# A planner that lets DVE's scales take turns with POOL, unit 0 ahead of unit 1 at the start, and new orders

## The chip, the cores and the metric

One core of one Trainium2 chip. The metric is the device time of one execution in microseconds. TensorE is called PE, VectorE DVE, ScalarE ACT, GpSimd POOL and SyncE SP. DVE's and POOL's elementwise work, ACT's activations, PE's matmuls and the DMA queues run side by side and wait for one another through semaphores.

## The reference, cut to what matters

Linear attention with a decay for each head (4 batches, 8 heads, 768 positions, 64 channels), then a feed-forward layer of width 2048 over the 3072 tokens of 512 channels:

```python
intra = np.einsum('bhic,bhjc->bhij', qb, kb) * Dmask[None]
intra = np.einsum('bhij,bhjd->bhid', intra, vb)
inter = np.einsum('bhid,bhde->bhie', qb * lam_pow[None], kv_state)
out[:, :, sl] = intra + inter
kv_state = lam_block * kv_state + np.einsum('bhsd,bhse->bhde', kb * rev_pow, vb)
...
h = x @ w_in                       # x: the attention's result, (3072, 512)
g = h + np.sin(alpha * h) ** 2 / (alpha + 1e-09)
return g @ w_out
```

## The kernel before, in words

The sequence is cut into blocks of 128 positions; two blocks of one batch are a unit, and there are 12. For each unit q, k and v come as float32 over SP's queue: in halves of four heads (256 KB) for units 0 and 1, whole (512 KB) for the others, into three buffers of each, so unit u's load waits until unit u-3's is used up. `uscale` (L504) turns each half into bfloat16: q and v are multiplied by powers of lambda (L523, "a scale"), k is only cast (L509). k and q are then transposed: by PE with a copy by DVE or ACT (`upiece_T`, L531) for units 0 to 3, by a DMA transpose on SP's queue (`upiece_D`, L552) from unit 4 on. `urun` (L583) issues the attention's small matmuls (L578) for units 0 to 3: S (scores of four heads, then masked by DVE into Smu, L658), Z (the new state: DVE keeps it in Zs, L669 and L671, and a cast Zu, L674, goes to PE), O (the outputs, which DVE or ACT writes to xT, L688). `upair` (L695) does all three for a whole unit from unit 4 on, the O of the unit before beside the S and Z of the next ("a paired piece").

Two units make a chunk of 512 tokens, six in all. For a chunk, an A-unit makes 128 rows of h from the first weights w1: four matmuls of 512 columns (`unit_A`, L811), or, as a half unit (`unit_A2`, L845), eight of 256 columns for 256 rows and half the tokens. Then ACT takes the sine (L821 or L855), ACT or POOL squares it (L825 and L859 on ACT, L826 and L860 on POOL), and DVE adds it to h into gT (L828 or L863). A B-unit (`unit_B`, L876) is four matmuls of gT with the second weights w2; four B-units make 128 tokens of output, which ACT copies (L890) and stores.

The weights come through POOL's queue as float32 and land as bfloat16, in pieces of a quarter: D0 to D3 for w1 (D0 is missing: its two halves, ws0 and ws256, come as float32 over SP's queue and are cast by `cast_w1_first`, W0 and W256, L424), E0 to E3 for w2. The text calls D1, D2, D3 weight pieces 1, 2, 3; E0 is the piece that the first B-units read. Each has a gate, written behind the colon in HEAD: `D3:v11` is issued once v of unit 1, half 1, has landed. Unit 2's loads wait for D3.

The program is made by a planner, `_Plan`. PE's and SP's instructions are issued in the order of the tables, except that the planner may take one of the next 40 on PE if it is ready sooner; ACT, DVE and POOL take whatever its model says is ready first, and where an operation names several engines (a scale, a square, an xT copy) the one that ends first, with a handicap for some. The durations are written beside each operation. From this the planner fixes every engine's order once; on the chip each engine runs its list in that order. Where PE would wait in the first 26 us the planner puts in spin matmuls (L950), which compute nothing that is used.

Two tables set the rest: HEAD (L437) is the start, with `lk00` the load of k of unit 0, half 0, `k00:DVE` its scale and engine, `Tk00` its transpose, `S0`, `Z0`, `O0`, `X0` the pieces of attention, `F:` the order of the free PSUM banks. ORDER (L899) is what follows: `h0.1.6` a half unit of chunk 0, half 1, rows of 6 and 7; `a0.4` an A-unit; `b0.2.0` a B-unit; `g` the next piece of attention; `s` skips a bank. Before, the loads, scales and DMA transposes of later units were called by a rule of their own (`ahead`, L980).

## Time and profile before

| | us |
|---|---|
| median of 3 runs | 216.63 |
| lowest, highest | 216.14, 216.72 |
| profiled execution | 216.58 |
| its span | 214.8 |
| busy: PE, DVE, ACT, POOL | 205.0, 136.6, 143.5, 93.9 |
| spin matmuls, part of PE's | 11.2 |
| PE idle from 25 to 60, 60 to 90, 90 to 200 | 0.98, 2.28, 0.07 |

The span is what the profiler saw of instructions. A group's row gives the line, the engine, the operation, output and inputs with their shapes and a count; behind the bar stand its busy time, the mean of one in ns, and the time that the engine was idle just before, with what ended it. The granted clock of TensorE is full throughout.

### The profile page before, as it was taken

Reading aid. Unit: us, or ns where it says so; the run is one execution under the profiler, and the core shown is the slowest. Engines: PE = TensorE matmul, PEld = TensorE weight load, DVE = VectorE, ACT = ScalarE, POOL = GpSimd, SP = SyncE. Lnnn points to the kernel's source line nnn. Section 1 sums busy time; section 2 is a strip of 40 time slices with the busy share of each in tenths; the row PEclk is TensorE's granted clock in tenths of the full one; section 3 lists DMA queues with packets and bytes.
Section 4 is the critical chain, followed back from the end, with each engine's and each line's share of the span. In section 5 each row is a group of like instructions: output and inputs, shape, how many; then the busy total and the mean of one; then the engine's idle time right before and its main releaser. Section 6 shows DMA issues by size and latency. Waiting matters only on the chain.

```text
span 214.8 us, 5435 instructions
## 1 busy us (share of the span) xinstructions
PE 205.0 (95%) x2290; PEld 114.9 (53%) x2290; DVE 136.6 (64%) x225; ACT 143.5 (67%) x264; POOL 93.9 (44%) x106
## 2 busy tenths in 40 slices
...
GB/s 108 298 309 234 206 255 258 252 265 344 297 202 289 271 179 318 178 283 218 277 251 268 99 49 101 2 42 62 0 52 49 0 0 3 0 2 49 52 146 148
DMA packets 62986, 34.45 MB, mean 160 GB/s; under 512 B 18273, under 2 KB 60017, under 8 KB 62961
## 3 DMA queue, kind: packets, MB, share of 16 engines
...
q0 software_dynamic: 3696, 3.67, 10.3%
...
## 4 chain that ended last, share of the span: by engine, by line
PE 78%; DMA 11%; POOL 3%; SPq 3%; ACT 2%; issue 1%; DVE 0%; POOLq 0%
PE bank L876 38%; PE bank L811 18%; PE bank L845 13%; PE bank L578 7%; DMA w<-in_moe_w_in_dram 5%; DMA k<-in_k_dram 3%; SPq L385 3%; DMA q<-in_q_dram 3%; POOL u L826 2%; PE bank L539 1%; POOL w L385 1%; ACT t L821 1%; POOL qkv L523 1%; ACT osb L890 0%; DVE gT L828 0%
## 5 line engine op out<-in xcount | busy, mean ns | idle before, releaser
L876 PE MATMUL bank<-w,gT 128*128 128x512 bf16 (+1 forms) x400 | 89.6, 371 | 1.0 <-ACT osb L890 0.7
L876 PEld LDWEIGHTS bank<-w,gT 128*128 128x128 bf16 x400 | 38.0, 98 | 41.6 <-ACT osb L890 1.2
L828 DVE SCALAR_TENSOR_TENSOR gT<-u,rinv,bank 128x512 bf16<-128x512 bf16 x56 | 40.7, 744 | 22.0 <-ACT u L825 13.4
L811 PE MATMUL bank<-xT,w 128*128 128x512 bf16 x224 | 53.1, 379 | 0.8 <-DVE gT L828 0.5
L821 ACT ACTIVATE t<-bank,alpha 128x512 bf16<-128x512 f32 x56 | 37.4, 685 | 12.2 <-PE bank L811 11.4
L863 DVE SCALAR_TENSOR_TENSOR gT<-u,rinv,bank 128x256 bf16<-128x256 bf16 x80 | 34.3, 475 | 12.8 <-POOL u L860 7.3
L845 PE MATMUL bank<-xT,w 128*128 128x256 bf16 x320 | 38.7, 273 | 0.2 <-DVE gT L828 0.2
L855 ACT ACTIVATE t<-bank,alpha 128x256 bf16<-128x256 f32 x80 | 32.9, 474 | 6.6 <-PE bank L845 5.0
L811 PEld LDWEIGHTS bank<-xT,w 128*128 128x128 bf16 x224 | 21.5, 98 | 25.7 <-DVE gT L828 1.0
L845 PEld LDWEIGHTS bank<-xT,w 128*128 128x128 bf16 x320 | 30.5, 98 | 8.2 <-ACT xT L788 1.5
L860 POOL TENSOR_TENSOR u<-t 128x512 bf16<-128x512 bf16 x25 | 26.0, 1056 | 17.8 <-ACT t L855 17.7
L826 POOL TENSOR_TENSOR u<-t 128x512 bf16<-128x512 bf16 x19 | 20.2, 1069 | 29.9 <-ACT t L821 19.6
L890 ACT COPY osb<-bank 128x512 f32<-128x512 f32 (+1 forms) x25 | 14.2, 568 | 21.9 <-PE bank L876 21.9
L767 DVE TENSOR_TENSOR Smu<-bank,masku 128x1024 bf16<-128x1024 f32 x16 | 18.9, 1219 | 13.6 <-PE bank L578 13.6
L825 ACT ACTIVATE u<-t 128x512 bf16<-128x512 bf16 x37 | 23.3, 630 | 1.8 <-DVE gT L828 0.6
L523 POOL TENSOR_TENSOR qkv<-v,Lv 128x512 bf16<-128x512 f32 x15 | 17.4, 1167 | 12.8 <-PE bank L578 10.9
L523 POOL TENSOR_TENSOR qkv<-q,Lq 128x512 bf16<-128x512 f32 x13 | 15.0, 1159 | 11.5 <-DMA q<-in_q_dram 11.5
L788 ACT CAST xT<-bank 128x512 bf16<-128x512 f32 x14 | 9.8, 740 | 9.5 <-PE bank L578 9.5
L950 PE MATMUL bank<-masku,ident 128*128 128x512 bf16 x33 | 11.2, 452 | 2.7 <-DVE masku L461 2.7
L658 DVE TENSOR_TENSOR Smu<-bank,masku 128x1024 bf16<-128x1024 f32 x8 | 9.7, 1223 | 3.3 <-PE bank L578 3.2
L509 ACT CAST qkv<-k 128x512 bf16<-128x512 f32 x11 | 6.8, 617 | 6.0 <-DMA k<-in_k_dram 6.0
L578 PE MATMUL bank<-qkT,Zu 64*64 64x128 bf16 x160 | 10.3, 221 | 0.3
...
## 6 DMA issues: line engine op xcount, KB each, us to landing
...
k<-in_k_dram SPq DMA_DIRECT2D x10, 512.0 KB, 6.5
q<-in_q_dram SPq DMA_DIRECT2D x10, 512.0 KB, 7.2
v<-in_v_dram SPq DMA_DIRECT2D x10, 512.0 KB, 8.0
w<-in_moe_w_out_dram POOLq DMA_DIRECT2D x4, 512.0 KB, 9.4
w<-in_moe_w_in_dram POOLq DMA_DIRECT2D x3, 512.0 KB, 11.4
...
```

Of the source, the lines that this page charges most:

```text
L523: emit = lambda e: e.tensor_tensor(dst, src, tab, ALU.mult)
L578: ins = e.matmul(to, w, x, start=(b, c) not in seen, stop=True, skip_group_check=True)
L811: ins = e.matmul(ps[hb][:, c0:c1], w1[:, kc, 128 * m:128 * (m + 1)], xT[x][:, kc, c0:c1], start=(kc == 0 and c0 == lo), stop=(kc == NKC - ...
L821: op("ACT", lambda e: e.activation(t16[ju][:, w], ps[hb][:, w], ACTF.Sin, scale=alpha[:, m:m + 1]), 0.69 * f, [bank(hb), "alpha"], [("t16" ...
L825: lambda e: (e.activation(u16[ju][:, w], t16[ju][:, w], ACTF.Square) if e is nc.scalar else e.tensor_tensor(u16[ju][:, w], t16[ju][:, w], ...
L826: e.tensor_tensor(u16[ju][:, w], t16[ju][:, w], t16[ju][:, w], ALU.mult)), 0,
L828: op("DVE", lambda e: e.scalar_tensor_tensor(out=gT[g][:, m, w], in0=u16[ju][:, w], scalar=rinv[:, m:m + 1], in1=ps[hb][:, w], op0=ALU.mul ...
L845: ins = e.matmul(ps[hb][:, 256 * i:256 * i + 256], w1[:, kc, 128 * (m + i):128 * (m + i + 1)], xT[x][:, kc, lo:lo + 256], start=(kc == 0 a ...
L855: op("ACT", lambda e, i=i: e.activation(t16[ju][:, 256 * i:256 * i + 256], ps[hb][:, 256 * i:256 * i + 256], ACTF.Sin, scale=alpha[:, m + ...
L860: e.tensor_tensor(u16[ju][:, :], t16[ju][:, :], t16[ju][:, :], ALU.mult)), 0,
L863: op("DVE", lambda e, i=i: e.scalar_tensor_tensor(out=gT[g][:, m + i, lo:lo + 256], in0=u16[ju][:, 256 * i:256 * i + 256], scalar=rinv[:, ...
L876: ins = e.matmul(ps[ob][:, w], gT[g][:, m, 128 * s4:128 * (s4 + 1)], w2[:, m, w], start=(m == 0), stop=(m == NM - 1),)
```

## The change

1. In the planner, the scales and k casts on DVE (`port = True`) may not run while POOL runs anything, nor POOL beside one of them: each starts only when the other's last has ended. This holds in the planner's model; on the chip nothing is added, only the choice of engine and the order follow from it.
2. HEAD is new: all loads of unit 0 but one come ahead of unit 1's, q first; ws0, the first half of the first weights, is loaded in the middle; the transposes of unit 1 are four single ones; both casts of the first weights go to DVE; D3 is gated by v of unit 0, D1 and D2 by ws0. The bank order is new.
3. ORDER is new. Loads (`l`), scales (`p`) and DMA transposes (`d`) of later units are tokens in it; 46 half units and 50 whole ones take the place of 40 and 56. Handicaps for ACT and DVE (`late_by`) are read from a token `G:` of HEAD. A few durations and landing times of the model are corrected.

```diff
+        ends = {"POOL": 0.0, "DVE": 0.0}
+        def free(o, e):
+            return max(clock[e], ends["DVE"] if e == "POOL" else ends["POOL"] if e == "DVE" and o.port else 0.0)
...
-                    _, e, d = min((max(r, clock[e]) + d + late, e, d) for e, d, late in o.given)
-                    c = (max(r, clock[e]), index[o], o, e, d)
+                    _, e, d = min((max(r, free(o, e)) + d + late, e, d) for e, d, late in o.given)
+                    c = (max(r, free(o, e)), index[o], o, e, d)
...
+            if e == "POOL" or e == "DVE" and o.port:
+                ends[e] = clock[e]
...
-            HEAD = """lk00 lv00 lq00 lk01 k01:POOL lv01 lq01 v01:POOL q00:POOL lk10 k00:DVE Tk00:7ACT lq10 lk11 Tq00:6DVE
+            HEAD = """lq01 lq00 lk00 lk01 k00:POOL q00:POOL lv00 Tk00:5DVE lv10 lv01 lq10 lw0 D1:w0 lk10 Tq00:6DVE
...
-                    long = {"POOL": 1.05 if u > 1 else 1.1, "DVE": 0.68}
+                    long = {"POOL": 1.04, "DVE": 0.68}
...
+                o.port = True
...
-                op((("POOL", 1.05 * f, 0.0), ("ACT", 0.6 * f, 0.2)),
+                op((("POOL", 1.05 * f, 0.0), ("ACT", 0.62 * f, late_by[0])),
...
-                while ahead and ahead[0][0] <= done:
-                    ahead.pop(0)[1]()
...
+                elif kind == "l":
+                    load_unit(next(loads), "kqv")
+                elif kind == "p":
+                    uprep(next(preps))
+                elif kind == "d":
+                    u = next(turns)
+                    upiece_D(u, "k")
+                    upiece_D(u, "q")
```

POOL at the start, from its first scale on. `q32_0` is q of unit 0, `q32_1` of unit 1; `w1` and `w2` are weight pieces; `dma_uv01` is the landing of v of unit 0, half 1, `dma_ws0` and `dma_ws256` of the two small loads of first weights. Before:

```order
L523 TENSOR_TENSOR qkv<-q32_0,Lq 128x2x4x64 [waits dma_uq00,done_ACT]
L509 CAST qkv<-k32_0 128x2x4x64 [waits dma_uk01]
L523 TENSOR_TENSOR qkv<-v32_0,Lv 128x512 [waits dma_uv01,done_ACT]
L523 TENSOR_TENSOR qkv<-q32_0,Lq 128x2x4x64 [waits dma_uq01]
L674 CAST Zu_0<-Zs 128x256 [waits done_DVE]
L385 DMA w1<-in_moe_w_in_dram 128x4x512 [waits dma_uq11]
L385 DMA w2<-in_moe_w_out_dram 128x4x512
L385 DMA w1<-in_moe_w_in_dram 128x4x512 [waits dma_uv11]
```

The changed POOL at the same place:

```order
L532 TENSOR_TENSOR qkv<-q32_0,Lq 128x2x4x64 [waits dma_uq01,done_ACT]
L532 TENSOR_TENSOR qkv<-q32_0,Lq 128x2x4x64 [waits dma_uq00]
L518 CAST qkv<-k32_0 128x2x4x64 [waits dma_uk00]
L532 TENSOR_TENSOR qkv<-v32_0,Lv 128x512 [waits dma_uv01,done_ACT]
L532 TENSOR_TENSOR qkv<-q32_1,Lq 128x2x4x64 [waits dma_uq10]
L393 DMA w1<-in_moe_w_in_dram 128x4x512
L393 DMA w1<-in_moe_w_in_dram 128x4x512 [waits dma_ws0]
L518 CAST qkv<-k32_1 128x2x4x64 [waits dma_uk10]
```

Unit 0's v and unit 1's first q now stand ahead of the first weight pieces; the piece with no wait of its own is D3, the next D1. Before, D1 came first, then E0, then D3.

PE at its first big matmuls, behind the first A-unit (a half unit) and the first output of unit 1. `xT_0` is the attention's result for chunk 0, `Smu_3` the last masked scores of unit 1, `masku,ident` a spin matmul. Before:

```order
L578 MATMUL bank<-Smu_3,qkv 64x128 [waits done_DVE]
L578 MATMUL bank<-Smu_3,qkv 64x128 x15
L578 MATMUL bank<-qkT,Zu_1 64x128 x2
L578 MATMUL bank<-qkT,Zu_1 64x128 [waits done_PE]
L578 MATMUL bank<-qkT,Zu_1 64x128
L845 MATMUL bank<-xT_0,w1 128x256 [waits done_ACT]
L845 MATMUL bank<-xT_0,w1 128x256 x7
L845 MATMUL bank<-xT_0,w1 128x256 [waits dma_w11,done_DVE]
L845 MATMUL bank<-xT_0,w1 128x256 x23
L811 MATMUL bank<-xT_0,w1 128x512 [waits done_DVE]
```

The changed PE there:

```order
L588 MATMUL bank<-Smu_3,qkv 64x128 [waits done_DVE]
L588 MATMUL bank<-Smu_3,qkv 64x128 x15
L588 MATMUL bank<-qkT,Zu_1 64x128 x2
L588 MATMUL bank<-qkT,Zu_1 64x128 [waits done_PE]
L588 MATMUL bank<-qkT,Zu_1 64x128
L962 MATMUL bank<-masku,ident 128x512 x4
L855 MATMUL bank<-xT_0,w1 128x256 [waits done_DVE,done_ACT]
L855 MATMUL bank<-xT_0,w1 128x256 x7
L821 MATMUL bank<-xT_0,w1 128x512 [waits dma_w11]
L821 MATMUL bank<-xT_0,w1 128x512 x3
```

Four spins now stand ahead of the second A-unit (a half unit), and the third, a whole one, waits for weight piece 1 (`dma_w11`); before, the third was a half unit that waits for the same piece, with no spin in between.

DVE in chunk 1's first A-units. `q32_2`, `k32_2` and `v32_2` are the third of three buffers, with unit 5 in them here; `gT_1` is chunk 1's g. Before:

```order
L863 SCALAR_TENSOR_TENSOR gT_1<-u16_1,rinv,bank 128x256
L523 TENSOR_TENSOR qkv<-q32_2,Lq 128x2x4x64 [waits dma_uq2]
L828 SCALAR_TENSOR_TENSOR gT_1<-u16_3,rinv,bank 128x512 [waits done_ACT]
L828 SCALAR_TENSOR_TENSOR gT_1<-u16_2,rinv,bank 128x512 [waits done_POOL]
L523 TENSOR_TENSOR qkv<-v32_2,Lv 128x512 [waits dma_uv2]
L828 SCALAR_TENSOR_TENSOR gT_1<-u16_0,rinv,bank 128x512 [waits done_ACT]
```

The changed DVE at the same place:

```order
L873 SCALAR_TENSOR_TENSOR gT_1<-u16_1,rinv,bank 128x256
L518 CAST qkv<-k32_2 128x2x4x64 [waits dma_uk2]
L873 SCALAR_TENSOR_TENSOR gT_1<-u16_2,rinv,bank 128x256 [waits done_POOL]
L873 SCALAR_TENSOR_TENSOR gT_1<-u16_2,rinv,bank 128x256
L873 SCALAR_TENSOR_TENSOR gT_1<-u16_3,rinv,bank 128x256 [waits done_POOL]
```

The two scales are gone from between the sums; a k cast is there instead. In the whole program DVE keeps two scales of 20, both in the start, and POOL has 46 where it had 28; ACT has 40 squares for 52.

82 lines of the change are left out of this document (41 added, 41 removed).

## The prediction

> **What bounds the kernel now.** I read the busy time by stretches first, since TensorE (PE) is busy 95% of the span and only its gaps can be won. Columns: stretch in us, its length, busy us of PE, PEld (weight loads), DVE, ACT, POOL, granted clock, DMA share, GB/s.
>
> ```profile
> 25.00:60.00 35.00, 34.02 (x420) 19.85 (x418) 27.76 (x47) 24.12 (x46) 20.71 (x22) 1.00 1.12 272
> 60.00:70.00 10.00, 8.66 (x87) 4.44 (x87) 8.49 (x15) 8.90 (x16) 7.71 (x9) 1.00 1.27 248
> ...
> 80.00:90.00 10.00, 9.06 (x216) 5.24 (x205) 6.40 (x8) 6.05 (x11) 4.62 (x5) 1.00 1.12 242
> 90.00:200.00 110.00, 109.93 (x1110) 60.91 (x1109) 69.29 (x112) 80.42 (x146) 43.02 (x46) 1.00 0.41 92
> ```
>
> From 90 to 200 PE idles 0.07 us: nothing there gets shorter without less PE work. The chain of work that ended last (start, us, what) gives that work by units:
>
> ```profile
> 90.23 0.87 PE bank L845 x8
> ...
> 92.83 0.86 PE bank L811 x4
> ```
>
> A half unit of eight matmuls lasts as long as a whole one of four, so six more of the one kind for six fewer of the other change PE's work by nothing. What can change is when useful work starts, 0.98 us of gaps from 25 to 60, 1.34 in the sixties, 0.94 in the eighties. Then I read the groups by line (the second number behind the bar is the mean in ns):
>
> ```profile
> L821 ACT ACTIVATE t<-bank,alpha 128x512 bf16<-128x512 f32 x56 | 37.4, 685 | 12.2 <-PE bank L811 11.4
> L855 ACT ACTIVATE t<-bank,alpha 128x256 bf16<-128x256 f32 x80 | 32.9, 474 | 6.6 <-PE bank L845 5.0 <-POOL qkv L523 1.3
> L860 POOL TENSOR_TENSOR u<-t 128x512 bf16<-128x512 bf16 x25 | 26.0, 1056 | 17.8 <-ACT t L855 17.7
> L523 POOL TENSOR_TENSOR qkv<-v,Lv 128x512 bf16<-128x512 f32 x15 | 17.4, 1167 | 12.8 <-PE bank L578 10.9 <-DMA v<-in_v_dram 1.9
> ```
>
> POOL's scales average 1.17 where the shortest rows have 1.04. The timeline (start, us, engine, line) shows why: scales of DVE and POOL that overlap run one behind the other.
>
> ```profile
> 53.84 1.04 POOL L523 TENSOR_TENSOR qkv<-q,Lq 128x512 bf16<-128x512 f32 x1
> 53.95 1.48 DVE L523 TENSOR_TENSOR qkv<-q,Lq 128x512 bf16<-128x512 f32 x1
> 54.84 1.49 POOL L523 TENSOR_TENSOR qkv<-v,Lv 128x512 bf16<-128x512 f32 x1
> ```
>
> DVE's scale ends at 55.43, 0.55 after POOL's first; POOL's second ends 0.90 after that. In the sixties such a pair stands in front of work that PE waits for:
>
> ```profile
> 59.17 6.22 PE L811 MATMUL bank<-xT,w 128*128 128x512 bf16 x28
> ...
> 63.98 1.20 DVE L523 TENSOR_TENSOR qkv<-v,Lv 128x512 bf16<-128x512 f32 x1
> 64.60 1.49 POOL L523 TENSOR_TENSOR qkv<-v,Lv 128x512 bf16<-128x512 f32 x1
> ...
> 65.90 1.04 PE L811 MATMUL bank<-xT,w 128*128 128x512 bf16 x4 [0.52 <-DVE gT L828]
> ...
> 67.34 0.44 PE L578 MATMUL bank<-qkv 64*64 64x64 bf16 x16 [0.40 <-DVE gT L863]
> ```
>
> **The sixties.** Between PE's first A-unit of chunk 1 and the paired piece of unit 4, I count what each order gives each engine, at these durations. Before: three half units and eight whole ones, 10.2 us of PE, against ACT 11.7, DVE 10.2 (three scales in it), POOL 9.9. Changed: six half, four whole and a B-unit, 10.3 of PE, against ACT 9.8, DVE 8.7 (no scale), POOL 11.3 (six scales, the last two needed only later). From 59.17 to 67.34 PE took 8.17 us for eight units worth 6.9; the piece then waits 0.4 and twice 0.2 more: 2.0 us lost. With ACT and DVE below PE most of this goes; for POOL, which stays above, I leave 0.5 lost: **-1.5**.
>
> **POOL's load.** 18 scales leave DVE and 12 squares leave ACT for POOL: 18 x 1.04 + 12 x 1.06, some 31 us on 93.9. In the sixteen A- and B-units from the 41st on, its count is 16.4 us against PE's 15.7, and squares stand behind pairs of scales (2.08). The trace shows no POOL that full beside a PE without gaps. Bounds: nothing (four buffers between ACT and POOL take it up; less than nothing isn't possible, since the relief is counted above) and 0.7 for the excess plus 0.8 for a square behind a pair. I take **+0.4**, near the low end, as both counts of ACT and DVE are smaller there. In the eighties PE waits mostly for ACT's copy of an output; ACT has some 10 us less to do, and I take back half of the 0.94: **-0.4**.
>
> **The head.** Useful work starts at 19.84, is continuous from 22.08, and stops twice:
>
> ```profile
> 19.84 1.04 PE L845 MATMUL bank<-xT,w 128*128 128x256 bf16 x8
> 22.08 3.73 PE L845 MATMUL bank<-xT,w 128*128 128x256 bf16 x32
> 31.38 1.04 PE L876 MATMUL bank<-w,gT 128*128 128x512 bf16 x4 [0.36 <-DVE gT L863]
> 34.69 0.61 PE L539 MATMUL bank<-ident,qkv 128*128 128x128 bf16 x8 [0.55 <-ACT qkv L509]
> ```
>
> The changed start I walk by hand. First the loads (7th and 9th in the queue of SP, then the 13th, a ws; then POOL's weight pieces, issue and us to landing; the last two are steps of the chain):
>
> ```profile
> 10.87 0.62 ACT L509 CAST qkv<-k 128x512 bf16<-128x512 f32 x1 [2.86 <-DMA k<-in_k_dram]
> 12.67 0.62 ACT L509 CAST qkv<-k 128x512 bf16<-128x512 f32 x1 [1.19 <-DMA k<-in_k_dram]
> 16.87 1.05 ACT L424 CAST w<-ws 128x1024 bf16<-128x1024 f32 x1 [0.67 <-DMA ws<-in_moe_w_in_dram]
> 13.89 0.94 POOL L385 DMA_DIRECT2D w<-in_moe_w_in_dram  x1 [2.19 <-DMA q<-in_q_dram]
> w<-in_moe_w_in_dram POOLq DMA_DIRECT2D x1, 512.0 KB, 7.9
> 15.56 11.39 DMA w<-in_moe_w_in_dram
> 26.97 6.94 DMA k<-in_k_dram
> ```
>
> A load lands every 0.9 us, a ws takes 1.5. Weight pieces land at 21.8 (13.89 + 7.9) and, the third, at 26.95: 2.55 apart. The second engine of the walk is DVE:
>
> ```profile
> L658 DVE TENSOR_TENSOR Smu<-bank,masku 128x1024 bf16<-128x1024 f32 x8 | 9.7, 1223 | 3.3 <-PE bank L578 3.2
> L688 DVE CAST xT<-bank 128x512 bf16<-128x512 f32 x4 | 2.8, 725 | 1.5 <-PE bank L578 1.5
> L509 DVE CAST qkv<-k 128x512 bf16<-128x512 f32 x3 | 1.3, 434 | 0.5 <-DMA k<-in_k_dram 0.5
> L669 DVE COPY Zs<-bank 128x256 f32<-128x256 f32 x2 | 0.9, 426 | 0.9 <-PE bank L578 0.9
> L548 ACT COPY qkT<-bank 128x512 bf16<-128x512 bf16 x1 | 0.6, 568 | 0.0
> ```
>
> In the new order the second v of unit 0 is the 7th load, 10.9; POOL ends it at 11.95 and unit 1's first q at 12.97, and only then issues weight piece 3, then piece 1. DVE: two Smu (1.22) from 10.95 to 13.4, two state copies to 14.2, the cast W0 (twice a k cast, an estimate of 0.85) to 15.05, xT to 15.8. This frees the bank for unit 1's k transposes; ACT's copy (0.57) and the score follow at 16.95, Smu_2 ends at 18.6, the scale of v at 19.3, unit 1's state at 20.3. The first A-unit uses the state's bank: **20.3**. Ahead of the second stand Smu_3 (to 21.5), W256 (22.4; its ws, the last load, should be there by 21.3 beside piece 3) and xT (23.1): **23.2**. Piece 3 is issued 0.92 earlier than the first piece was, but into the same bytes, so I leave the landings where they were: 3 near 21.8, piece 1 at 24.35, piece 2 at 26.95. The third unit waits for piece 1; the third to fifth run from 24.35 to 24.35 + 3 x 0.87 = 26.95, and the sixth needs piece 2: **27.0**. Before, five units from 19.84 and 22.08 on brought the sixth to 25.6: 1.4 late. Then something comes back: piece 3 releases unit 2's loads, at 21.8 and not at 26.97. Its k, 6.9 us later, is there at 29 and even four us later still ahead of its transposes, due some 9 us after the sixth unit; so the stops of 0.36 and 0.55 go. That leaves 0.5, and I add 0.1 for squares held up behind POOL's issues: **+0.6**.
>
> The unknown is how unit 2's loads and pieces 2 and E0 slow each other. Below: not at all, and DVE's chain 0.6 shorter, as its estimates allow: 0. Above: as the last two pieces of before, which ran beside them:
>
> ```profile
> 30.35 0.81 POOL L385 DMA_DIRECT2D w<-in_moe_w_out_dram  x1
> 34.19 0.81 POOL L385 DMA_DIRECT2D w<-in_moe_w_out_dram  x1 [1.68 <-DMA k<-in_k_dram]
> w<-in_moe_w_out_dram POOLq DMA_DIRECT2D x2, 512.0 KB, 9.1
> ```
>
> They land near 39.5 and 43.3, 3.8 apart: 1.25 more than 2.55 for each of two pieces, +2.5 on 0.6. I stay near the low end, since by 26.95 unit 2's loads have moved for only three us.
>
> Nine more spin matmuls stand only where PE would wait for the walk above, and cost nothing as long as it does.
>
> **Sum**, against the profiled execution of 216.58 (span 214.8 and 1.8 around it; the median of the runs is 216.63): +0.6 - 1.5 + 0.4 - 0.4 = -0.9, **215.7**.
>
> **A rule against the change.** A weight piece's issue on POOL took 0.94 at 13.89, beside DVE's scales, and 0.75 here, beside another:
>
> ```profile
> 14.81 0.68 DVE L523 TENSOR_TENSOR qkv<-v,Lv 128x512 bf16<-128x512 f32 x1
> 14.82 0.75 POOL L385 DMA_DIRECT2D w<-in_moe_w_out_dram  x1
> ```
>
> By these rows an overlap costs 0.2 at most. The Trainium skill (SBUF — State Buffer, section "SBUF: two separate sides") says that GpSimd can't write descriptors while VectorE runs a 2-port operation such as an fp32 copy within SBUF, so that its DMA starves. By the rows the sum stays 215.7, by that rule it is the fourth rival's; the row at 14.82 does not show it.
>
> **The rivals.** (1) *Weights too late* (slower): unit 2's loads, released at 21.8, run against pieces 2 and E0. It decides once piece 2 lands after 28; then the sixth unit and the first B-unit each wait 1.25 more, and POOL, whose next issue waits for piece 2, holds a square (1.06) behind it, half of which PE feels: -0.9 + 2.5 + 0.5 = +2.1, 218.7 at the full price, 217.7 at half. For it speaks the 9.1; against it that nothing else runs until 23. (2) *Everything goes*: the head costs 0, the sixties give 2.0, the eighties 0.9, POOL costs 0.2: -2.7, 213.9. For it speak the counts of ACT and DVE. (3) *The scales weren't it*: ACT made the sixties (8.90 busy of 10) and goes on doing so, since a half unit takes twice 0.474 of it where a whole one takes 0.685; -1.5 becomes -0.6: 216.6, no change. (4) *Starved descriptors*: DVE's new cast W0, near 14.2, holds the issue of piece 1 for its whole 0.85, and the third to sixth units with it: 216.5. The 0.75 beside 0.68 speaks against it, the 0.94 for a little of it. The rule of the Trainium skill above would make it so.
>
> **How the numbers follow.** Forecast 0.42 (215.0 to 216.4, a sixth of it within 0.3% of no change), weights too late 0.27, everything goes 0.17, scales weren't it 0.10, starved 0.04. A measurement of this kernel can tell about 0.3%, 0.65 us, from no change. Faster: 0.35 + 0.17 = 0.52; same: 0.07 + 0.10 + 0.04 = 0.21; slower 0.27. The range takes in the fast rival and the slow one to between its half and full price: 213.8 to 218.2.
>
> **What would show it.** POOL's scales with a mean near 1.05 and no q scale on DVE; the first A-unit at 20.3, the second at 23.2, the third released by a weight piece's landing; piece 3 landing first, near 21.8, and k of unit 2 before 33; no wait at unit 2's transposes; under 0.6 us of PE gaps in the sixties' A-run. The forecast is wrong if PE waits for a weight piece after 27.5, or if PE idles while DVE waits for POOL's squares.

## The result, and the profile after

The changed kernel takes **217.1 us** (median of 21 runs, 216.04 to 219.71) where the kernel before took 216.12 beside it (21 runs, 215.94 to 216.76): a ratio of 1.0042 [1.0031, 1.0053], slightly slower. The forecast was 215.7: the sign was wrong. Medians are over all executions, ratios leave the disturbed ones out; the first profile of the changed kernel fell in a disturbed execution (219.7), so the one read here is the first experiment's, of the same kernel: 217.05 beside a median of 217.04, span 215.3.

The busy time by stretches of the changed kernel, with the columns and stretches of the prediction:

```profile
25.00:60.00 35.00, 32.98 (x406) 19.27 (x410) 20.55 (x34) 22.84 (x44) 25.04 (x28) 1.00 1.16 266
60.00:70.00 10.00, 9.91 (x113) 6.70 (x115) 8.40 (x16) 8.66 (x18) 9.46 (x10) 1.00 0.97 234
...
80.00:90.00 10.00, 9.01 (x239) 5.69 (x239) 5.71 (x7) 4.27 (x8) 4.27 (x6) 1.00 0.95 233
90.00:200.00 110.00, 108.78 (x1115) 62.33 (x1126) 65.97 (x112) 76.47 (x140) 57.67 (x65) 1.00 0.42 98
```

PE is busy 9.91 of the ten sixties, where it was 8.66: the change does what it was counted on for. But from 25 to 60 its busy time leaves 2.02 where it left 0.98, and the eighties are as they were. (Not all of what is missing is idle time: the page of this trace has 2300 matmuls for 2323 weight loads, so some matmul records are missing. From 25 to 60 the waits in the timeline below come to 1.33; PE's 108.78 from 90 on is no idle time either, as the markers below show that stage no longer than before.) The groups of POOL in the changed kernel, squares and scales:

```profile
L870 POOL TENSOR_TENSOR u<-t 128x512 bf16<-128x512 bf16 x40 | 40.8, 1040 | 10.7 <-ACT t L865 9.4 <-DVE gT L838 1.1
L532 POOL TENSOR_TENSOR qkv<-q,Lq 128x512 bf16<-128x512 f32 x24 | 25.0, 1058 | 5.8 <-ACT Lq L481 3.8 <-DMA q<-in_q_dram 1.9
L532 POOL TENSOR_TENSOR qkv<-v,Lv 128x512 bf16<-128x512 f32 x22 | 22.5, 1042 | 6.7 <-PE bank L588 3.5 <-DMA v<-in_v_dram 3.2
```

A scale takes 1.04 to 1.06 and not 1.17. What PE waited for between 20 and 130 us (engine and line, for what; us in total, times, longest), first before:

```profile
PE bank L876 <- ACT osb L890: 0.7, 1, 0.7
PE bank L539 <- ACT qkv L509: 0.5, 1, 0.5
PE bank L811 <- DVE gT L828: 0.5, 1, 0.5
PE bank L578 <- DVE gT L863: 0.4, 1, 0.4
PE bank L876 <- DVE gT L863: 0.4, 1, 0.4
```

and the same view of the changed kernel:

```profile
PE bank L549 <- POOL qkv L532: 0.7, 1, 0.7
PE bank L886 <- ACT osb L900: 0.7, 1, 0.7
PE bank L886 <- issue: 0.5, 3, 0.2
PE bank L588 <- issue: 0.4, 1, 0.4
PE bank L855 <- DMA w<-in_moe_w_in_dram: 0.2, 1, 0.2
```

The waits for DVE's gT are gone. New are a wait for POOL's scale of a load (L549), one for a weight piece (L855), and one, at L588, for nothing that the profile shows; together 1.3, less than what went. (The row of L886 with "issue" is no wait: it is three places where one matmul record of a group is missing.) So part of the loss must lie where PE's waits don't show, since spins fill them: ahead of 27 us. I compared the times at which the two programs reach the same amount of work: PE instructions that have the same A- and B-units ahead of them in both orders (start of the instruction in both timelines, us).

| place | before | changed | difference |
|---|---|---|---|
| first A-unit | 19.84 | 20.73 | +0.89 |
| sixth unit | 25.65 | 27.76 | +2.11 |
| unit 2's state sums, 16 A-units and 7 B-units ahead | 43.65 | 45.77 | +2.12 |
| 32 A, 23 B ahead | 79.43 | 80.37 | +0.94 |
| 32 A, 26 B ahead | 84.47 | 85.45 | +0.98 |
| 54 A, 48 B ahead | 128.04 | 128.63 | +0.59 |
| last instruction of PE | 212.19 | 212.70 | +0.51 |

The changed kernel loses 2.1 in the head and wins back 1.2 between 45 and 80: 1.6 less a new stop of 0.41. The 0.4 won from 85 to 128 is mostly a stop of 0.27 that the profiled execution of before had there. That execution (216.58) lay 0.46 above its median of 216.12, which is most of the way from +0.51 between the two profiles to +0.98 between the medians.

Where in the head? First one line of PE's timeline before, unit 2's state sums:

```profile
43.65 0.45 PE L578 MATMUL bank<-qkv 64*64 64x64 bf16 x32
```

and PE's timeline in the changed kernel (start, us; in brackets the idle time ahead and who ended it):

```profile
20.73 1.05 PE L855 MATMUL bank<-xT,w 128*128 128x256 bf16 x8
...
23.87 1.05 PE L855 MATMUL bank<-xT,w 128*128 128x256 bf16 x8
24.97 0.81 PE L821 MATMUL bank<-xT,w 128*128 128x512 bf16 x3
...
27.76 1.05 PE L855 MATMUL bank<-xT,w 128*128 128x256 bf16 x8 [0.23 <-DMA w<-in_moe_w_in_dram]
...
41.55 0.62 PE L549 MATMUL bank<-ident,qkv 128*128 128x128 bf16 x8 [0.69 <-POOL qkv L532]
...
45.77 0.45 PE L588 MATMUL bank<-qkv 64*64 64x64 bf16 x32
...
52.24 0.27 PE L588 MATMUL bank<-qkT 64*64 64x128 bf16 x6
52.93 0.35 PE L588 MATMUL bank<-qkT 64*64 64x128 bf16 x10 [0.41 <-issue]
```

At 41.55 are unit 2's q transposes, where the prediction wrote "no wait". They waited for POOL's two scales of q, which waited for the landing of q, in POOL's timeline:

```profile
39.45 2.04 POOL L532 TENSOR_TENSOR qkv<-q,Lq 128x512 bf16<-128x512 f32 x2 [1.34 <-DMA q<-in_q_dram]
```

The chain of the changed kernel (start, us, what) does not go through this stop but through the load behind q, v, whose scales release unit 2's sums at 45.77:

```profile
12.89 9.16 DMA w<-in_moe_w_in_dram
...
23.10 20.51 DMA v<-in_v_dram
...
43.68 2.05 POOL qkv L532 x2
...
45.77 0.67 PE bank L588 x48
```

The chain runs from piece 3's issue over its landing at 22.05, which releases unit 2's loads, to v. That load is issued 3.9 us **earlier** than the k that led the chain before (26.97) and lands 20.51 us later, at 43.61. PE reached the sums at about 45.6, so without the stop of 0.69 at q it would have stopped nearly as long for v: both loads have to come earlier. The issue of each load and its flight, for q before and then in the changed kernel, are in the view of one tile (duration in ns, start):

```profile
L385 SPq DMA_DIRECT2D q<-in_q_dram x1: 585/585/585, 27.4 to 27.4; - x1
...
DMA to landing us min/median/max: 8.1/8.1/8.1
```

```profile
L393 SPq DMA_DIRECT2D q<-in_q_dram x1: 583/583/583, 22.5 to 22.5; - x1
...
DMA to landing us min/median/max: 16.9/16.9/16.9
```

The same for all of them, from the DMA records of both traces (issue and landing, us):

| | before | changed |
|---|---|---|
| weight pieces in order of issue: landing | 21.82, 24.36, 26.95, 29.45, 32.57, then 39.53, 43.22 | 22.05, 24.59, 27.71, 31.36, 35.05, 38.69, 43.12 |
| sixth piece (E2): issue | 30.35 | 28.00 |
| k of unit 2 | 26.97, 33.91 | 22.07, 33.76 |
| q of unit 2 | 27.38, 35.45 | 22.48, 39.38 |
| v of unit 2 | 28.00, 41.83 | 23.10, 43.61 |

Before, the weight pieces pause between E1 and E2: from 30 to 34 the trace has 81 packets of pieces beside 2266 of loads. k and q fly in the pause and land 1.54 apart. In the changed kernel the five pieces land later, beside the loads, and E2 is issued 2.35 earlier, right when piece 2 has landed, so a piece is in flight without a break from 13 to 43; from 30 to 34 there are 462 packets of pieces beside 1027 of loads. A whole load takes some 1.5 behind another where no piece is in flight, and 4.2 to 6.4 beside one; a piece takes 2.55 alone and 3.1 to 4.4 beside a load.

### The profile page after: what moved, and what is told of

It reads as the page before. It is cut to its first block, busy times and chain, and to the rows that moved or that the text cites. A ratio compares the mean times of both kernels' runs of the same rounds, so it can differ in the third digit from the quotient of the medians.

```text
span 218.0 us, 5499 instructions
## 1 busy us (share of the span) xinstructions
PE 209.0 (96%) x2323; PEld 120.2 (55%) x2323; DVE 127.8 (59%) x218; ACT 133.6 (61%) x252; POOL 120.3 (55%) x139
## 4 chain that ended last, share of the span: by engine, by line
PE 91%; DVE 2%; DMA 2%; POOL 2%; ACT 1%; issue 0%
PE bank L886 37%; PE bank L821 20%; PE bank L855 19%; PE bank L588 10%; PE bank L962 4%; PE bank L549 2%; DMA lam_bc<-in_lam_dram 2%; POOL qkv L532 1%; DVE w L432 1%; POOL u L870 0%; ACT osb L900 0%; ACT t L865 0%; DVE xT L698 0%; DVE Zs L679 0%; DVE Zs L681 0%
## 5 line engine op out<-in xcount | busy, mean ns | idle before, releaser
L886 PE MATMUL bank<-w,gT 128*128 128x512 bf16 (+1 forms) x400 | 89.0, 371 | 0.7 <-ACT osb L900 0.7
L886 PEld LDWEIGHTS bank<-w,gT 128*128 128x128 bf16 x400 | 38.3, 98 | 41.1 <-ACT osb L900 1.2
L838 DVE SCALAR_TENSOR_TENSOR gT<-u,rinv,bank 128x512 bf16<-128x512 bf16 x50 | 36.2, 745 | 29.6 <-ACT u L835 21.9
L870 POOL TENSOR_TENSOR u<-t 128x512 bf16<-128x512 bf16 x40 | 40.8, 1038 | 17.8 <-ACT t L865 16.0
L821 PE MATMUL bank<-xT,w 128*128 128x512 bf16 x200 | 47.0, 379 | 0.0
L873 DVE SCALAR_TENSOR_TENSOR gT<-u,rinv,bank 128x256 bf16<-128x256 bf16 x92 | 39.8, 476 | 12.1 <-POOL u L870 8.0
L865 ACT ACTIVATE t<-bank,alpha 128x256 bf16<-128x256 f32 x92 | 37.9, 472 | 10.2 <-PE bank L855 8.7
L855 PE MATMUL bank<-xT,w 128*128 128x256 bf16 x368 | 44.0, 273 | 0.0
L855 PEld LDWEIGHTS bank<-xT,w 128*128 128x128 bf16 x368 | 35.0, 98 | 8.8 <-ACT xT L798 0.9
L836 POOL TENSOR_TENSOR u<-t 128x512 bf16<-128x512 bf16 x16 | 16.4, 1039 | 26.8 <-ACT t L831 26.1
L532 POOL TENSOR_TENSOR qkv<-q,Lq 128x512 bf16<-128x512 f32 x24 | 24.9, 1056 | 3.8 <-ACT Lq L481 3.8
L532 POOL TENSOR_TENSOR qkv<-v,Lv 128x512 bf16<-128x512 f32 x22 | 22.5, 1041 | 5.9 <-PE bank L588 3.6
L962 PE MATMUL bank<-masku,ident 128*128 128x512 bf16 x42 | 15.0, 480 | 2.7 <-DVE masku L470 2.7
L791 POOL CAST Zu<-Zs 128x256 bf16<-128x256 f32 x11 | 4.3, 398 | 18.8 <-DVE Zs L788 14.1
L588 PE MATMUL bank<-qkT,Zu 64*64 64x128 bf16 x160 | 10.3, 221 | 0.4
```

Of the source, the lines that this page charges most:

```text
L532: emit = lambda e: e.tensor_tensor(dst, src, tab, ALU.mult)
L588: ins = e.matmul(to, w, x, start=(b, c) not in seen, stop=True, skip_group_check=True)
L821: ins = e.matmul(ps[hb][:, c0:c1], w1[:, kc, 128 * m:128 * (m + 1)], xT[x][:, kc, c0:c1], start=(kc == 0 and c0 == lo), stop=(kc == NKC - ...
L838: op("DVE", lambda e: e.scalar_tensor_tensor(out=gT[g][:, m, w], in0=u16[ju][:, w], scalar=rinv[:, m:m + 1], in1=ps[hb][:, w], op0=ALU.mul ...
L855: ins = e.matmul(ps[hb][:, 256 * i:256 * i + 256], w1[:, kc, 128 * (m + i):128 * (m + i + 1)], xT[x][:, kc, lo:lo + 256], start=(kc == 0 a ...
L865: op("ACT", lambda e, i=i: e.activation(t16[ju][:, 256 * i:256 * i + 256], ps[hb][:, 256 * i:256 * i + 256], ACTF.Sin, scale=alpha[:, m + ...
```

## The experiments

Theories at the start. **Shared wire**: unit 2's loads land late since they share the transfers with weight pieces in flight; take the pieces away or move them, and the stop at 41.55 goes. **Cast**: W0 on DVE holds POOL's issue of pieces and delays the head. **Tables**: HEAD itself or ORDER itself is slower. **Instructions**: the 0.41 at 52.93 is PE waiting for its own instructions. Ratios are to the kernel before, run beside them, with their 95% interval.

| experiment | median us | ratio |
|---|---|---|
| e1_after | 217.04 | 1.0054 [1.0029, 1.0080] |
| e2_w0_act | 216.54 | 1.0017 [1.0004, 1.0030] |
| e3_old_head | 220.66 | 1.0213 [1.0187, 1.0239] |
| e4_new_head | 224.95 | 1.0421 [1.0395, 1.0448] |
| e5_light_weights | 216.11 | 1.0013 [0.9993, 1.0034] |
| e6_gate_d2 | 217.98 | 1.0093 [1.0056, 1.0131] |
| e7_no_gate | 218.67 | 1.0104 [1.0079, 1.0130] |
| e8_q_on_act | 216.61 | 1.0015 [1.0000, 1.0031] |
| e9_after_spin | 217.56 | 1.0062 [1.0048, 1.0076] |
| e10_w0_act_spin | 217.35 | 1.0050 [1.0033, 1.0067] |
| e11_q_act_spin | 218.11 | 1.0056 [1.0022, 1.0090] |
| e12_cast_in_row | 216.67 | 1.0032 [1.0013, 1.0051] |
| e13_e2_later | 216.34 | 1.0018 [1.0004, 1.0032] |
| e14_e2_latest | 216.32 | 1.0003 [0.9993, 1.0012] |
| e15_after_e2_later | 216.39 | 1.0017 [0.9998, 1.0037] |
| e16_after_few_spins | 217.73 | 1.0084 [1.0071, 1.0098] |
| e17_e14_few_spins | 217.24 | 1.0045 [1.0026, 1.0064] |

Medians and ratios don't rank alike where a kernel's executions spread (e5's lie near 215.95 and near 217.5). A profile is one execution out of these. Most edits are made in the planner's finished list: the line that settles it becomes `order = self.late_edit(self._settle())`, and the diffs below show the body of `late_edit`; `last["k", 2]` is the load of unit 2's k, `last["w1", 3]` piece 3, `last["w2", 2]` E2.

### The changed kernel again, and W0's cast on ACT

e1_after is the changed kernel without an edit. Its expectation starts from the first profile, in which W0's cast took 2.99.

> The changed kernel once more, for a profile beside the others of this chip. Theory 'cast' (DVE's cast W0 can't go on while POOL runs its row of scales, 2.99 us where 0.69 is its time alone; everything behind it in the head is late): the cast takes 2.5 us or more again, the first A-unit of chunk 0 starts after 23 us, and the sixties have under 0.6 us of PE gaps. Rival 'weights' (weight pieces D1 and D2 set the start): the cast's length varies, but the third A-unit starts with a landing of D1 and not with DVE. About 217 us either way.

e2_w0_act changes one engine, and no order moves besides:

```diff
-   q01:POOL S0:4 lq11 lv11 k01:DVE v00:DVE F:1506743 v01:POOL lk11 v11:POOL W0:DVE k10:POOL Z0:5
+   q01:POOL S0:4 lq11 lv11 k01:DVE v00:DVE F:1506743 v01:POOL lk11 v11:POOL W0:ACT k10:POOL Z0:5
```

> The changed kernel with the cast W0 on ACT (1.05 us there) in place of DVE; nothing else moves on any engine. Theory 'cast': xT and the whole walk behind it come 2 to 3 us earlier, the first A-unit starts near 20.5 to 21.5, and 1 to 2 us of it reach the end: 215.1 to 216.1. Rival 'weights': the third unit waits for D1 as before the edit, the end moves by less than 0.3: 216.8 to 217.3. Rival 'order' (what is lost is lost behind the head, by the new order of the A-run): also within 0.3.

The cast, in DVE's timeline of the changed kernel, runs from 13.81 on:

```profile
13.81 0.69 DVE L432 CAST w<-ws 128x1024 bf16<-128x1024 f32 x1
```

POOL issues piece 3 and piece 1 from 12.89 on, beside it; in POOL's timeline of the changed kernel, and then of e2_w0_act:

```profile
12.89 1.91 POOL L393 DMA_DIRECT2D w<-in_moe_w_in_dram  x2
```

```profile
12.87 1.68 POOL L393 DMA_DIRECT2D w<-in_moe_w_in_dram  x2
```

So the cast took 0.69 and the first A-unit began at 20.73: theory 'cast' of e1, 2.5 or more and an A-unit after 23, fell for this execution. The two issues take 0.23 more beside the cast, piece 2 lands at 27.71 and not at 27.52, and PE's 0.23 at 27.76 goes. So a cast on DVE does make POOL's issue longer, by 0.23 and not by its whole length. The median falls by 0.5, which none of the three forecasts of e2 had; the profile of e2 also lacks the 0.41 at 52.93, so the two can't be told apart by the medians alone. The late loads are untouched (q lands at 39.44, v at 43.45), and the stop at q's transposes is 0.95.

### Is it one of the tables?

e3_old_head puts before's HEAD, with its bank order and with the token `G:` that the new planner reads, into the changed kernel; e4_new_head puts the new HEAD without that token into the kernel before. The first line of the edit of e3; in e4 it goes the other way:

```diff
-   HEAD = """lq01 lq00 lk00 lk01 k00:POOL q00:POOL lv00 Tk00:5DVE lv10 lv01 lq10 lw0 D1:w0 lk10 Tq00:6DVE
+   HEAD = """lk00 lv00 lq00 lk01 k01:POOL lv01 lq01 v01:POOL q00:POOL lk10 k00:DVE Tk00:7ACT lq10 lk11 Tq00:6DVE
```

> The old order of the head (W0 and W256 on ACT, both units' loads in turn, D1 first) with the changed planner and the new order of all that comes behind. Theory 'cast': the sixties keep their gain (under 0.6 us of PE gaps between 60 and 70) and the head starts at 19.8 as before the change: 214.8 to 215.8. Rival 'order': the new order behind the head costs the time, 216.8 or more.

> The kernel before the change with the new head alone (old planner, old order behind the head). Theory 'cast': the cast W0 is long here too, and the loss of the head stands without the gain of the sixties: 218 to 219.5. Rival 'order': the new head costs nothing, 216.3 to 216.9.

Both are far slower than their parents, e4 beyond both its forecasts and e3 by more than its rival needed, by stops that neither parent has. PE's timeline of e3_old_head, and of e4_new_head:

```profile
50.78 0.88 PE L548 MATMUL bank<-ident,qkv 128*128 128x128 bf16 x8 [1.83 <-DVE gT L837]
```

```profile
47.53 0.62 PE L540 MATMUL bank<-ident,qkv 128*128 128x128 bf16 x8 [2.71 <-DVE gT L829]
```

Head and order are made for one another, so these two do not say what either is worth. One thing can be read: in e4, with before's ORDER, unit 2's loads land at 33.78, 38.66 and 43.14, as late as in the changed kernel. The late landings come with the head.

### Fewer weight bytes

e5_light_weights is e2 with E2 and E3 cut to a quarter, so that part of the output is computed from other rows of the second weights:

```diff
-   w2[:, 4 * i:4 * i + 4, :],
-   moe_w_out[512 * i:512 * (i + 1), :]
+   w2[:, 4 * i:4 * i + (4 if i < 2 else 1), :],
+   moe_w_out[512 * i:512 * i + (512 if i < 2 else 128), :]
...
-   gT[g][:, m, 128 * s4:128 * (s4 + 1)], w2[:, m, w],
+   gT[g][:, m, 128 * s4:128 * (s4 + 1)], w2[:, m % 8, w],
```

> The kernel of e2 (cast W0 on ACT), every instruction in the same place, with three quarters of the weight pieces E2 and E3 left out (128 of 512 rows are loaded, and the B-units use the rows of E0 and E1 in their place, so part of the output is computed from other weights). Theory 'wire' (from 22 to 43 us unit 2's loads share the DMA engines with six weight pieces, so that an early release doesn't bring them earlier; q of unit 2 lands at 39.4 and stops PE at its transposes, v at 43.6 decides when unit 2's state sums start): unit 2's q lands before 38.0 and its v before 41.0, the stop of 0.95 at the transposes of q goes, unit 2's state sums start 0.7 to 1.1 earlier than e2's 45.61, and the end is 0.5 to 1.1 under e2's 216.54: 215.4 to 216.0. Rival 'POOL' (POOL comes late to the scales of q because of its squares, whatever the landings are): q lands earlier, but the stop stays over 0.5 and the end within 0.3 of e2.

q lands at 36.68 and v at 38.31, where they landed at 39.44 and 43.45 in e2, and there is no stop at q's transposes: the weight pieces are what the loads waited behind, and the rival 'POOL' fell. The time does not show it (1.0013 beside e2's 1.0017, where 0.5 to 1.1 less was expected), and unit 2's sums start at 45.62, no earlier than e2's 45.61. In this execution (217.9) the first A-unit came only at 22.10, so PE itself was late for the sums, and it has a longer stop at the same score matmuls as e1, in PE's timeline of e5:

```profile
53.63 0.35 PE L588 MATMUL bank<-qkT 64*64 64x128 bf16 x10 [1.28 <-issue]
```

### Is it the moment of the release?

e6_gate_d2 is e2 with unit 2's loads behind piece 2, which lands at 27.07 there, nearly before's 26.97; e7_no_gate is e2 with no gate at all.

```diff
+   last["k", 2].deps.remove(last["w1", 3])
+   last["k", 2].deps.add(last["w1", 2])      # e6 alone
```

> The kernel of e2, every instruction in the same place; unit 2's loads wait for weight piece D2 (27.5) in place of D3 (21.9), which gives them back the release that they had before the change (26.97). Theory 'wire': D2 lands 0.4 to 0.9 earlier without them beside it, k, q and v of unit 2 land within 1.0 of where they did (33.8, 39.4, 43.6) though they are issued 5 us later, and the end is within 0.4 of e2. Rival 'release' (the forecast's own step: 6.9 us after issue, as in the kernel before): k lands at 34, no worse, but with an early release it would have been 29; q and v move 3 us or more later and the end is over 1.5 later.

> The kernel of e2, every instruction in the same place; unit 2's loads wait for no weight piece and go out behind the last load of the head, near 12.5 us. Theory 'wire': all three land 5 us or more earlier (v before 38), the weight pieces D1, D2 and E0 pay for it with 1 to 4 us each, the sixth A-unit waits for D2 until 29 or later, and the end is 0.5 to 2.5 later than e2. Rival 'release': the loads come early, the pieces keep their times, and the end is 0.9 earlier than e2.

In e6 the loads are issued from 27.09 on, as in the kernel before, yet k lands at 36.80 (33.91 before), q at 38.34 and v at 39.98: E2 is issued at 27.36 there and flies beside k. So before's quick k was not a matter of its release. But the wire theory had put the loss of e6 within 0.4, and that fell: PE stops at unit 2's k transposes, in the timeline of e6,

```profile
39.12 0.62 PE L549 MATMUL bank<-ident,qkv 128*128 128x128 bf16 x8 [2.92 <-POOL qkv L518]
```

and the kernel is 1.4 us slower than e2. One microsecond behind the stop the granted clock falls to half, from 40.1 to 43.5 in the trace's records, so this execution (219.73) shows more than the stop. When the loads go decides which piece each flies beside, and who is late. In e7 k lands first, at 27.33, and the pieces pay: piece 1 at 26.53, piece 2 at 30.12, E0 at 33.85. PE's timeline of e7:

```profile
26.80 0.81 PE L821 MATMUL bank<-xT,w 128*128 128x512 bf16 x3 [1.90 <-DMA w<-in_moe_w_in_dram]
...
30.16 1.05 PE L855 MATMUL bank<-xT,w 128*128 128x256 bf16 x8 [0.80 <-DMA w<-in_moe_w_in_dram]
```

That is the first rival of the prediction as it was written, weights too late, and it is 2 us slower than e2. The new gate of unit 2's loads at piece 3 lies between two worse ones.

### Another queue for q

e8_q_on_act is e2 with unit 2's q issued on ACT's queue at 23.0.

```diff
+   o = last["q", 2]
+   o.eng = "ACT"
+   o.deps.add(last["w1", 3])
+   order.remove(o)
+   order.insert(next(i for i, x in enumerate(order) if x.eng == "ACT" and x.start > 22.4), o)
```

> The kernel of e2, every instruction in the same place, but the load of q of unit 2 is issued by ACT at 22.7 us, in a DMA queue of its own, so that two of unit 2's loads and the weight pieces take turns three ways. Theory 'wire' with turns by queue: q lands 3 us or more earlier (under 36.5), pieces E0 to E2 1 to 2 us later, within their slack; the stop at the transposes of q goes, and the end is 0.4 to 1.0 under e2: 215.5 to 216.1, under the kernel before. Rival 'bytes' (the sum of bytes alone decides): q and v land where they did, no change within 0.3.

q lands at 36.48 (39.38 in the changed kernel), the stop at its transposes is gone, and the time is e2's, not 0.4 to 1.0 less. This execution lost time at the very start, in PE's timeline of e8, against that of the changed kernel below it (unit 0's first transposes):

```profile
7.09 0.61 PE L549 MATMUL bank<-ident,qkv 128*128 128x128 bf16 x4 [0.77 <-POOL qkv L532]
```

```profile
6.99 0.40 PE L549 MATMUL bank<-ident,qkv 128*128 128x128 bf16 x4 [0.67 <-POOL qkv L532]
```

The same transposes took 0.6 in that execution and 0.4 in the other, and the first A-unit began at 21.91 and not at 20.73. The orders up to there are the same. So PE was late for unit 2's sums by itself: they began at 45.44, in e2 at 45.61.

### The slow start of PE, and the cast again

A new question, and a theory for it: PE starts cold when it idled ahead of the transposes, so a ninth spin matmul in the first group (and nothing else) cures it. e9_after_spin puts it into the changed kernel, e10_w0_act_spin into e2, e11_q_act_spin into e8. e12_cast_in_row adds to e9 that W0's cast stands behind the xT copy in DVE's order, away from the issue of the pieces.

```diff
+   f = next(o for o in order if o.eng == "PE")
+   f.emit = lambda h, b=f.emit.__defaults__[0], n=f.emit.__defaults__[1] + 1: spin(h, b, n)
+   o = next(o for o in order if ("w1", 0) in o.writes and ("ws", 0) in o.reads)      # e12 alone, to the end
+   order.remove(o)
+   order.insert(order.index(made["xT", 0]) + 1, o)
```

> The changed kernel with one more spin matmul (nine in place of eight) in PE's first idle stretch, which ends at the transposes of q at 7.0 us. Theory 'cold start': in the trace of the changed kernel that fell behind, PE's matmuls between 7 and 11.9 us took 1.5 times as long (four transposes 0.61 to 0.64 in place of 0.40), DVE reached W0 at 15.2 in place of 13.8, inside POOL's row, and the cast took 2.99 in place of 0.69; the gap of 0.67 ahead of 7.0 decides whether that happens. With the gap filled, the transposes take 0.40 by 8.0 us at the latest, the cast starts before 14.2 and takes 0.69, and the runs lie closer together: none above 218, median 216.5 to 217.0. Rival 'chance elsewhere': the spread and the median stay (217.04, up to 219.6).

> The kernel of e2 (cast W0 on ACT) with the ninth spin. Theory 'wire': a late start of the head is hidden by the landing of unit 2's q (39.4), so the spin changes the median by less than 0.3: 216.2 to 216.8. Rival 'cold start' alone: 0.5 or more faster, 216.0 or less.

> The kernel of e8 (q of unit 2 in ACT's queue) with the ninth spin. e8's profiled run had the slow start (first A-unit at 21.9 in place of 20.7) and still reached unit 2's sums at 45.44, e2 with the quick start at 45.61. Theory 'wire' and 'cold start' together: with both out of the way the first A-unit starts at 20.7, PE doesn't stop at the transposes of q, unit 2's sums start 44.4 to 44.9, and the end is 0.5 to 0.9 under e2: 215.6 to 216.1, level with the kernel before or under it. Rival: v's landing (41.8) and POOL's scales of it hold unit 2's sums at 45.3 or later, no gain.

> The kernel of e9 with DVE's cast W0 one place later, behind xT, so that it starts at 15.6, in the middle of POOL's four scales and casts (14.8 to 18.0). Theory 'port' (DVE's cast out of SBUF can't run while POOL works through its row): the cast takes 2.0 us or more, until POOL turns to its DMA issue near 17.7 to 18, the copy of unit 1's k behind it on DVE starts 1 us or more later than 17.06, the first A-unit at 21.7 or later, and the end is 0.3 to 2 us over e9's. Rival: two instructions share the port in turn, the cast takes under 1.4 us, nothing behind it moves by more than 0.5.

The theory fell. None of the three is faster than its parent without the spin, and each median lies above both its forecasts (e9's profiled execution took 543.8 and is not read), and the gap ahead of the transposes does not decide it: 0.78 in e10, which started quick, 0.39 in e11, which started slow. The first four transposes take 0.40 or 0.61 in quick starts too (0.61 in e2, e7 and e15); what tells the two apart is the three groups behind, all at 0.40 in e1, e2, e6, e7, e10, e12 and e15, with the first A-unit between 20.5 and 20.8, and at 0.63 or 0.64 in e8, e11 and e14, with the first A-unit between 21.9 and 22.3. In e13 the last of them takes 0.46, and the A-unit begins at 21.68.

The traces' records of the granted clock say what a slow start is. They begin with a full clock at 5.5 to 7.5 us in the quick starts e2, e6, e7, e10 and e15, and only at 10.5, 11.2, 11.7 and 12.0 in the slow ones e13, e8, e14 and the first profile (e1, e11 and e12 have none); e13's transposes, 0.63 at 9.07, take 0.46 at 10.35. e5 has the same pace under a clock that is on record: 0.40 at 8.25, and 0.56 and 0.63 in the stretch from 8.9 to 12.3 that the records give as 0.50. So in a slow start the transposes take what they take at half the granted clock, and in e13 that ends where the full clock begins. Where nothing is recorded the profile's rows print 1.00; in the kernel before that holds up to 7.75, and its transposes at 6.00 take 0.61. Why the full clock comes later in some executions stays open. Nor is it shown that a slow start costs time at the end: e13's execution, a slow one, is the fastest of its eleven (215.95).

e12 tells how a cast and POOL meet when POOL computes. DVE's timeline of e12, then POOL's:

```profile
15.53 1.22 DVE L432 CAST w<-ws 128x1024 bf16<-128x1024 f32 x1
```

```profile
16.15 1.50 POOL L532 TENSOR_TENSOR qkv<-v,Lv 128x512 bf16<-128x512 f32 x1
```

Ahead of the second row POOL's scale of q runs from 15.15 to 16.20, at its usual 1.05. The cast, begun while it runs, ends 0.55 behind it, and the scale of v ends 0.90 behind the cast: the same 0.55 and 0.90 as in the pair at 53.84 in the prediction. So cast and scales ran one behind the other, which is e12's rival and not the theory that the cast waits until POOL's row is over. But the first profile has that too: its cast began at 15.23, again while POOL's scale of q ran, and took 2.99, until 0.55 behind the last of POOL's row (17.67), with the copy xT behind it and a wait of PE of 1.77 for that. No run here shows what gives the cast its turn. In e12 the first A-unit is not later for it (20.75), and the median is 0.4 below e1's.

### E2 later

If the piece that flies beside q is E2, it can be moved alone. e13_e2_later is e2 with E2's issue three POOL operations later (31.90 and not 27.81), e14_e2_latest five later (34.32, just ahead of E3); e15_after_e2_later makes e13's edit in the changed kernel.

```diff
+   o = last["w2", 2]
+   pool = [x for x in order if x.eng == "POOL"]
+   order.remove(o)
+   order.insert(order.index(pool[pool.index(o) + 3]) + 1, o)      # 5 in e14
```

> The kernel of e2, every instruction in the same place but one: POOL issues weight piece E2 behind three more squares, at 30.9 in place of 27.8 us. Theory 'wire': E2's transfer starts 2 to 3 us later, behind a stretch without a piece after E1's landing (34.9) in which q of unit 2 flies in; q lands at 35.0 to 37.0 (39.4 in e2), v before 42.5, E2 at 40 to 42, early enough for the B-unit that needs it near 43.5; the stop of 0.95 at the transposes of q goes, unit 2's sums start at 44.5 to 45.0 (45.61), the end is 0.4 to 1.0 under e2's 216.54: 215.5 to 216.1. Rival 'sum of bytes': q lands 39 or later again, the stop stays, no change within 0.3.

> As e13, but E2 goes out behind all five squares, right ahead of E3, at 33.0 to 33.8. Theory 'wire': q lands by 36, v by 39; E2 lands at 42 to 43.5 and E3 at 45.5 to 47, and now the B-units that need them wait: the stop at the transposes of q goes, but up to 1.5 us of stops on weight pieces come in between 43 and 49; the end between 0.8 under and 0.7 over e2. Rival 'sum of bytes': as e2 within 0.3.

> The changed kernel itself (cast W0 on DVE) with e13's one move. Theory 'wire': the same gain as e13 has over e2, 0.4 to 1.0 under the changed kernel's 217.04: 216.0 to 216.6, level with the kernel before or up to 0.5 over it. Rival 'sum of bytes': 216.8 to 217.3.

q lands at 35.95 in e13, 35.77 in e14 and 36.67 in e15, 2.5 to 3.1 behind k where it was 5.6, and in none of them is there a wait at its transposes; rival 'sum of bytes' fell. POOL's timeline of e13 shows E2's issue and, with no wait ahead of it, the scale of q:

```profile
31.90 0.81 POOL L393 DMA_DIRECT2D w<-in_moe_w_out_dram  x1
...
38.37 2.03 POOL L532 TENSOR_TENSOR qkv<-q,Lq 128x512 bf16<-128x512 f32 x2
```

and PE's timeline of e13 has both places free:

```profile
41.04 0.61 PE L549 MATMUL bank<-ident,qkv 128*128 128x128 bf16 x8
...
45.25 0.45 PE L588 MATMUL bank<-qkv 64*64 64x64 bf16 x32
```

Unit 2's sums start at 45.25 although this execution's first A-unit came only at 21.68. Its chain holds neither a load nor a weight piece from there on; ahead of the sums it goes through POOL, whose scales of v now stand behind a square:

```profile
21.68 1.05 PE bank L855 x8
...
42.16 1.04 POOL u L870
43.19 2.01 POOL qkv L532 x2
```

So the landings of q and v are put right by one piece issued 4 us later: the cause of the stop is shown. In e15, where E2 goes 2.8 later, v still lands at 43.23, and the stop only moves from q to v, in PE's timeline of e15:

```profile
45.40 0.45 PE L588 MATMUL bank<-qkv 64*64 64x64 bf16 x32 [0.91 <-POOL qkv L532]
```

What the landings are worth in time is less clear. On the changed kernel the move gains what was expected, 217.04 to 216.39 in the median and 1.0054 to 1.0017, most of the loss, though the two intervals overlap. On e2 it gains nothing that can be told from no change: e13 and e14 are 0.2 below e2 in the median, but their ratios are 1.0018 and 1.0003 beside e2's 1.0017, and 0.4 to 1.0 had been expected of e13. e14 is level with the kernel before, and no version is faster than it. The markers say why: unit 2's sums start at 45.25 in e13 and 45.59 in e14, still 1.6 and 1.9 behind the 43.65 of before, about what the sixties give back.

### The stop on instructions

e15's profiled execution (217.64) has the stop at unit 3's scores at its longest, in PE's timeline:

```profile
53.46 0.35 PE L588 MATMUL bank<-qkT 64*64 64x128 bf16 x10 [1.32 <-issue]
```

It stands ahead of the same matmul in e1 (0.41), e5 (1.28), e7 (0.69) and e15; in e10, with one spin more ahead, one matmul earlier, 0.78 in its timeline of PE:

```profile
53.04 0.36 PE L588 MATMUL bank<-qkT 64*64 64x128 bf16 x11 [0.78 <-issue]
```

A place fixed by the count of PE's instructions, and not by any work, is what a theory of instruction loading (called fetch) expects. The last packet of 16 KB on the instruction queue ends 1.41 ahead of the resumption in e1 (51.52 to 52.93), 1.42 in e7, 1.51 in e5, 1.58 in e15, 1.60 in e10, and 1.44 at before's stop of 0.27 (88.40 to 89.84). e16_after_few_spins and e17_e14_few_spins take 18 of the 42 spins out of the changed kernel and out of e14, which shifts PE's list against everything else.

```diff
+   fewer = [4, 3, 2, 2, 4, 3]
+   for f in [o for o in order if o.eng == "PE" and o.reads == ("masku", "ident") and o.start > 10.0]:
+       b, n = f.emit.__defaults__
+       if n > 2:
+           f.emit = lambda h, b=b, n=n - fewer.pop(0): spin(h, b, n)
```

> The changed kernel with 18 fewer of its 42 spin matmuls (those between 10.8 and 24 us; all other instructions in the same place). Theory 'fetch' (PE stops at a fixed number of its own instructions, when a packet of them comes late): no stop after the sixth of unit 3's sixteen score matmuls; a stop, if there is one, stands 18 matmuls later, among the B-unit's matmuls, and is about 0.9 shorter, mostly nothing; the median comes 0.3 to 0.6 under the changed kernel's 217.04: 216.4 to 216.7, if the idle PE of the head doesn't slow down (its four transposes stay at 0.40). Rival 'DMA or engine': the stop stands at the same matmul of the scores as before.

> e14's kernel (cast W0 on ACT, weight piece E2 late) with the same 18 spin matmuls left out: the three findings together. Theory 'fetch' with 'wire': 215.6 to 216.2, 0.1 to 0.7 under e14's 216.32 and level with the kernel before or under it (216.1). Rival: PE, idle in more of the head, runs its matmuls there at the slow rate, the first A-unit comes 1 us later and the end is 216.4 to 217.5.

The scores run without a stop in both, as expected, but a stop appears elsewhere, and the forecasts of the time were missed. PE's timeline of e16, and of e17:

```profile
91.51 1.68 PE L886 MATMUL bank<-w,gT 128*128 128x512 bf16 x7 [1.26 <-issue]
```

```profile
97.21 1.05 PE L855 MATMUL bank<-xT,w 128*128 128x256 bf16 x8 [1.19 <-issue]
```

with a packet ending 1.39 and 1.25 ahead. A count settles what the place goes by. PE's weight loads ahead of the stop (PEld in the view by stretches, from 0 to the stop) are 602 in e1, e5, e7, e10 and e15, although e10 has a spin more; 1109 in the kernel before and in e16, two different orders; and 1236 in e17. They lie 507 and 127 apart, four times some 127 and once. So the stops stand at places of PE's list some 127 matmuls with their weight loads apart, whatever work is there; only some of these places stop, and only in some executions. Leaving out spins moved other work to these places and removed no stop. Both kernels are slower than their parents by 0.7 and 0.9, though not all of that need be the stop: the head's waits are now idle ones, and in e16 the granted clock is at half from 16.4 to 19.8. The Trainium skill (Runtime: NRT & Kernel Launch, section "Instruction fetch mechanics") says that each engine's instructions are refilled in blocks of 16 KiB, 256 instructions, by a DMA queue of its own, and that crossing a block is "mostly hidden". The 16 KB packets agree, and so does the distance: 256 instructions are 128 matmuls with a weight load each, an estimate by that page's figure. Hidden it is in most crossings here (18 packets in a trace, and one stop at most), but not in all: it cost 0.27 to 1.32 where it was not.

## Why the prediction was wrong

By its own steps, against the profiled executions:

| term | predicted | measured | from |
|---|---|---|---|
| head | +0.6 | +2.1 | 43.65 to 45.77 |
| sixties | -1.5 | -1.6 | the fall from +2.12 to +0.94 at 80, without the next row's stop |
| stop at unit 3's scores | no step | +0.4 | 0.41 at 52.93 |
| POOL's load | +0.4 | 0 | no wait of PE for gT from 20 to 130 |
| eighties | -0.4 | 0 | wait for ACT's copy: 0.7 in both |
| 85 to 128 | no step | -0.4 | +0.98 to +0.59 |

**The head is the step that failed**, in two places, both for the same reason: what flies beside what. The walk itself held for long: the second score of unit 1 at 16.95 as walked, the first A-unit at 20.73 for 20.3, the second at 23.87 for 23.2, the third right behind it (piece 1 lands at 24.59 for 24.35, so it was there before it was needed). Then "the sixth needs piece 2: 27.0" came at 27.76, as piece 2 landed 0.76 later than written: 0.2 from the cast beside POOL's issue (e2), the rest since it came 3.12 behind piece 1 and not 2.55, with k in flight beside it (2.59 in e6, where the loads wait for it). And the sentence that fell is "Its k, 6.9 us later, is there at 29 and even four us later still ahead of its transposes ... so the stops of 0.36 and 0.55 go". They went; k, 11.7 us in flight, was in time, though at 33.76 and not by the 33 that was to show it. But q and v, of which the sentence did not speak, flew 16.9 and 20.5 us, and a stop of 0.69 at q's transposes came in place of the two. The forecast's own sign that it is wrong came true as well: PE waited 0.23 for piece 2, at 27.76. In sum: 1.4 + 0.7 at the sixth unit, 0.9 back, 0.7 lost again, and 0.2 of small gaps make the 2.1 that 0.6 was written for.

The error behind it: 6.9, 8.1 and 13.8 us were taken as the price of the loads, when they were the price of loads that fly in a pause of the weight pieces. The upper bound asked what the loads would cost the pieces (1.25 each) and never what the pieces would cost the loads. e5, e13, e14 and e15 show that: with E2 small or later, q lands 2.5 to 3.1 behind k and not 5.6. They show the cause of the landings and of the stop; that earlier landings win time is borne out on the changed kernel (e15) and not on e2 (e13). And most of the 2.1 is there by the sixth unit, which no profile with both new tables has before 27.3. The Trainium skill (DMA: Bandwidth & Descriptors, section "Queues, rings and completion order") says that each transfer engine goes round between the queues that have work, a packet at a time. The trace agrees: in each microsecond from 26 to 30 it counts 138 to 150 packets of loads beside 138 to 147 of pieces.

**Rival 1**, weights too late, had the right wire and the wrong victim: piece 2 at 27.71 did not pass its threshold of 28, and the pieces' delay cost PE 0.2; the loads paid. e7 is what it would have looked like. Half of its price of 3.0 on -0.9 is 217.2, not the 217.7 that it gives; that the measured 217.1 lies there, and inside the range, is luck, since what it names did not happen. **Rival 2** had the sixties near its 2.0 at 1.6, and nothing else. **Rival 3** fell: with the scales gone the sixties are full at an ACT busy 8.66 of 10. **Rival 4** was real and small in this execution, 0.23 of the 0.85. It leaned on the rule of the Trainium skill (SBUF — State Buffer, section "SBUF: two separate sides") that a copy on VectorE can keep GpSimd from writing descriptors; the rows agree in direction and do not show an issue held for a whole cast.

**Right** were the sixties (the scales' move and the new ORDER came together, and no run here tells which of the two filled them), POOL's scales at 1.04 to 1.06, no q scale on DVE, and piece 3 first near 22. **POOL's load** was feared for nothing: with 120.7 us busy for 93.9, PE's waits name neither POOL's squares nor gT. **The eighties** gave nothing, though ACT has 9.6 us less to do: the wait is for one copy of an output, and ACT had been idle for 2.68 just before.

What stays open: of the 0.5 between e1 and e2 at the medians, how much is the cast and how much the stop on instructions; why the full clock is granted later in some executions; what decides when DVE's cast gets its turn beside POOL's row; and which of the instruction places stops in which execution.
